# Two layers and a set of transposes put on 64-column tiles of TensorE, the shape that the projections beside them have

## The chip, the cores and the metric

The kernel runs on one core of a Trainium2 chip. The metric is device microseconds (us) of one execution. The span that a profile counts is about 2 us shorter than the timed execution. A time is called fast state where repeated executions agree within 1.5% and the granted clock is full; a single run of a one-core program has no state that could be told, and I use single runs below only for what their traces show or for differences far larger than the scatter.

## The reference

Attention with projected keys and values (Linformer), then a two-layer network on its output. There are 8 batches with 8 heads, 1024 positions and 64 values per head.

```python
k_proj = einsum('ks,bhsd->bhkd', E, k)            # 1024 positions -> 64
v_proj = einsum('ks,bhsd->bhkd', F, v)
attn   = softmax(q @ k_proj^T / 8) @ v_proj
x = attn.transpose(0, 2, 1, 3).reshape(8192, 512)
h = x @ w_in                                       # 512 -> 2048
g = h * clip(h + 3, 0, 6) / 6
out = g @ w_out                                    # 2048 -> 512, float32
```

## The kernel before

Inputs are cast to bf16 on their way in; sums are kept in f32 in PSUM. Each batch is two blocks of 512 tokens. The order of instructions on every engine is fixed by hand: the second layer of one block alternates with the first layer of the next, and the attention of the next batch is put between them in small pieces. TensorE's work has three main shapes: the layers use the full array (128 rows x 128 columns), the projections use two tiles of 128 x 64, and scores, values and most sums of attention use tiles of 64 x 64 (some sums use 128 x 32, and the first transposes of the keys 64 x 128). These are the parts that the change touches:

```python
def project(self, alloc):                 # 128x64, two column tiles in turn
    ps = self.ps = alloc()
    for so in range(SO):                  # SO = 8
        for e in range(2):                # 0: keys by E, 1: values by F
            nc.tensor.matmul(ps[e * KP:(e + 1) * KP], ef_t[e][:, so, :],
                             kqv[self.b]["kv"[e]][:, :, so, :],
                             start=(so == 0), stop=(so == SO - 1))
...
def queries(self, t, js):                 # first batch only
    ...
    nc.tensor.transpose(ps[:, o:o + P], q0[...], ident)
...
def h_part(h_ps, xT, t, fo, kos):         # first layer, 128x128
    for ko in kos:
        nc.tensor.matmul(h_ps, w_in_sb[:, ko, fo * P:(fo + 1) * P], xT[:, ko, t, :],
                         start=(ko == 0), stop=(ko == KO - 1))
...
def second_group(b, t, g, c, copy=None):  # second layer, 128x128
    ...
    for fo in range(FO):                  # FO = 16
        nc.tensor.matmul(o_ps, g[:, fo, c * P:(c + 1) * P], w_out_sb[:, fo, :],
                         start=(fo == 0), stop=(fo == FO - 1))
        if fo % SB == SB - 1:
            yield                         # attention may be put in here
```

Three more places matter for the experiments: the warm-up of TensorE at the start, the transfers that bring keys and queries into the layout for the scores, and where the next batch's work is put into the schedule of the first batch:

```python
busy(12)                                  # 12 matmuls of 512 columns on ones, before any data
...
def turn(self):                           # a transfer that transposes
    nc.sync.dma_start_transpose(self.kT, self.kp.rearrange("p h a d -> p (h a d)"))
    ...
    qT_dma[self.b] = q_transposed(self.b)
    ...
    nc.gpsimd.tensor_copy(mark, last)     # waits for qT; then the next batch is loaded
    load_kqv(self.b + 1, ...)
...
for fo in range(2, FO):
    first_group(xT, 1, g[1], fo)
    pop()
    if fo == 7:
        second.projected()                # projections of batch 1, and turn() afterwards
    ...
...
for c in range(SB):
    for i, _ in enumerate(second_group(0, 1, g[1], c, nc.vector.tensor_copy)):
        pop()
        if i == 0:
            rest.append(second.visit(c, None))   # visit(0): scores of batch 1
        ...
```

The softmax here doesn't subtract the row's maximum and nothing guards it: scores larger than these inputs give would overflow.

## Time and profile before

The first three runs gave a median of 507.31 us (507.19 to 507.36).

| | before |
|---|---|
| span in the profile | 505.3 us, granted clock 1.0 |
| TensorE busy | 495.5 us, 98% |
| ScalarE / VectorE busy | 256.2 us (51%) / 245.3 us (49%) |
| data moved | 66 MB, 131 GB/s on average |

In the lines of the profile PE is TensorE's matmuls, PEld its weight loads, DVE VectorE, ACT ScalarE, POOL GpSimd and SP SyncE; L532 is a line of the kernel, `a<-b` a tile and what it is made from, 128\*64 the rows and columns of the array that are used. The prediction below shows the lines for TensorE. Two more lines of the page of before also belong here. The first is the mean busy share of the 16 DMA engines in 40 slices of the span (in tenths, one slice is 12.6 us); the second is the queue on which TensorE's instructions come in: packets, MB, share of 16 engines.

```profile
DMA  9999989699199998699217990248110361101112
...
q8 instruction: 21, 0.34, 0.3%
```

In the first 80 us nearly every slice is at 9: the DMA engines have hardly a pause, so I take it that the transfers of that time land as late as the bandwidth makes them. The second line looks like nothing, and I read it so.

The view of the waits of TensorE in before (who waited for whom: us in total, times, longest) has six entries, of which these are the last three:

```profile
PE at L414 <- ACT vp L385: 0.5, 1, 0.5
PE mm L407 <- DVE kT L377: 0.3, 1, 0.3
PE mm L532 <- DVE g L503: 0.2, 1, 0.2
```

None of the six is a wait for a transfer. What the list doesn't say is by how little a transfer was in time.

### The profile page before, as it was taken

The numbers are of one execution on the slowest core, as the hardware profiler recorded it, in microseconds if no ns is written. First come the engines' busy times: TensorE is split into PE (matmuls) and PEld (weight loads), VectorE is DVE, ScalarE is ACT, GpSimd is POOL, SyncE is SP. The second block draws the span as 40 slices with busy tenths as digits, with TensorE's granted clock in tenths as the row PEclk, the third lists the DMA queues.
The fourth block names the chain that finished last, engine by engine and source line by source line (L and its number), as shares of the span: only waits on it lengthen the run. The fifth ranks groups of instructions, "written<-read, shape, count | busy, mean of one in ns | idle before, by whom it ended". The sixth has DMA issues, their size and how long they took to land.

```text
span 505.3 us, 7033 instructions
## 1 busy us (share of the span) xinstructions
PE 495.5 (98%) x2728; PEld 224.9 (45%) x2778; DVE 245.3 (49%) x384; ACT 256.2 (51%) x438; POOL 38.7 (8%) x58
## 2 busy tenths in 40 slices
PE   8899999999999999999999999999999999999997
PEld 4444444444444444444444444444444444444444
DVE  3572736855733573526635455533752446334420
ACT  3757476567574444654555544654455544434431
POOL 8620020010020020010002000000000000000000
PEclk9999999999999999999999999999999999999999
DMA  9999989699199998699217990248110361101112
GB/s 168 198 205 208 195 154 231 123 162 204 61 159 198 260 153 161 137 169 257 98 43 134 215 263 28 62 97 209 42 43 30 82 162 43 40 24 42 43 42 83
DMA packets 78057, 66.02 MB, mean 131 GB/s; under 512 B 36216, under 2 KB 67192, under 8 KB 78024
## 3 DMA queue, kind: packets, MB, share of 16 engines
q0 software_dynamic: 32480, 29.36, 37.1%
q1 hardware_dynamic: 45320, 35.89, 27.1%
q8 instruction: 21, 0.34, 0.3%
q10 hardware_dynamic: 224, 0.33, 0.3%
q14 instruction: 12, 0.10, 0.1%
HBM read 69.73 MB, written 16.94 MB: 172 GB/s over the span
## 4 chain that ended last, share of the span: by engine, by line
PE 97%; ACT 1%; issue 1%; DVE 0%; ACTq 0%
PE mm L532 43%; PE mm L497 43%; PE at L195 2%; PE mm L93 1%; PE at L244 1%; PE at L226 1%; PE mm L244 1%; PE mm L524 1%; PE mm L264 1%; PE at L414 1%; ACT aT L235 0%; PE mm L226 0%; PE at L382 0%; PE at L394 0%; PE mm L195 0%
## 5 line engine op out<-in xcount | busy, mean ns | idle before, releaser
L503 DVE SCALAR_TENSOR_TENSOR g<-r,mm 128x512 bf16<-128x512 f32 x256 | 173.6, 687 | 178.9 <-ACT r L502 178.1
L497 PE MATMUL mm<-xT,w_in_sb 128*128 128x512 bf16 x997 | 229.0, 379 | 1.5
L532 PE MATMUL mm<-w_out_sb,g 128*128 128x512 bf16 x985 | 227.8, 379 | 1.9 <-issue 1.0
L502 ACT ACTIVATE r<-mm 128x512 f32<-128x512 f32 x256 | 152.3, 599 | 74.5 <-PE mm L497 73.2
L497 PEld LDWEIGHTS <-w_in_sb 128*128 128x128 bf16 x1024 | 99.5, 98 | 122.2 <-issue 3.3
L532 PEld LDWEIGHTS <-g 128*128 128x128 bf16 x1008 | 96.7, 98 | 120.6 <-issue 7.4
L537 ACT COPY o_sb<-mm 128x512 f32<-128x512 f32 x55 | 32.3, 587 | 126.6 <-PE mm L532 123.7
L257 DVE TENSOR_TENSOR xT<-at,rec 128x512 bf16<-128x512 f32 x42 | 26.5, 682 | 6.4 <-ACT rec L176 6.4
L235 ACT ACTIVATE aT<-at 128x512 bf16<-128x512 f32 x38 | 20.2, 615 | 9.1 <-PE at L226 9.1
L201 DVE CAST kp<-at 64x512 bf16<-64x512 f32 x12 | 7.7, 677 | 15.5 <-PE at L195 15.5
L216 POOL COPY mark<-qT 1x1 bf16<-1x1 bf16 x4 | 0.7, 176 | 161.9 <-DMA qT<-q 161.9
L235 ACT ACTIVATE aT<-mm 128x512 bf16<-128x512 f32 x18 | 10.3, 613 | 3.6 <-PE mm L226 3.6
L537 DVE COPY o_sb<-mm 128x512 f32<-128x512 f32 x8 | 5.5, 688 | 13.4 <-PE mm L532 13.4
L195 PE MATMUL at<-k,e_t 128*64 128x512 bf16 x48 | 11.5, 382 | 0.0
L195 PE MATMUL at<-v,f_t 128*64 128x512 bf16 x48 | 11.5, 381 | 0.0
L257 DVE TENSOR_TENSOR xT<-mm,rec 128x512 bf16<-128x512 f32 x14 | 9.0, 686 | 4.3 <-PE mm L244 4.3
L176 ACT ACTIVATE rec<-rec 128x1024 f32<-128x1024 f32 x10 | 10.6, 1060 | 0.3
L170 ACT ACTIVATE rec<-mm 128x512 f32<-128x512 f32 x10 | 5.5, 595 | 7.9 <-PE mm L244 5.4
L170 ACT ACTIVATE few<-mm 128x512 f32<-128x512 f32 x10 | 5.4, 595 | 7.4 <-PE mm L264 7.4
L93 PE MATMUL mm<-ones 128*128 128x512 bf16 x18 | 7.4, 549 | 1.5 <-DVE halves L84 1.5
L204 DVE CAST vp<-at 64x512 bf16<-64x512 f32 x12 | 8.3, 694 | 0.4
L195 PEld LDWEIGHTS <-e_t 128*64 128x64 bf16 x56 | 5.6, 109 | 6.2 <-issue 1.9
(75 smaller groups left out, 161.0 us busy)
## 6 DMA issues: line engine op xcount, KB each, us to landing
out_dram<-o_sb SPq DMA_DIRECT2D x63, 256.0 KB, 2.5
rec<-rows SPq DMA_DIRECT2D x40, 256.0 KB, 6.2
k<-in_k_dram POOLq DMA_DIRECT2D x7, 1024.0 KB, 14.1
v<-in_v_dram POOLq DMA_DIRECT2D x7, 1024.0 KB, 20.9
q<-in_q_dram POOLq DMA_DIRECT2D x7, 1024.0 KB, 10.7
w_out_sb<-in_moe_w_out_dram POOLq DMA_DIRECT2D x4, 512.0 KB, 16.3
w_in_sb<-in_moe_w_in_dram POOLq DMA_DIRECT2D x5, 256.0 KB, 9.8
k<-in_k_dram POOLq DMA_DIRECT2D x4, 256.0 KB, 5.6
```

The costliest lines, as they stand in the source:

```text
L93: nc.tensor.matmul(ps, ones[:, :P], ones, start=True, stop=True)
L170: nc.scalar.activation(rec[:, i], den, AF.Ln)
L176: nc.scalar.activation(flat, flat, AF.Exp, scale=-1.0)
L195: nc.tensor.matmul(ps[e * KP:(e + 1) * KP], ef_t[e][:, so, :], kqv[self.b]["kv"[e]][:, :, so, :], start=(so == 0), stop=(so == SO - 1))
L235: nc.scalar.activation(self.aT[j][:, r].rearrange("p a n -> p (a n)"), tiles[r], AF.Exp, scale=scale)
L244: nc.tensor.matmul(tiles[t][c:c + D].rearrange("p (r n) -> p r n", r=2), stationary(r, 2 * j + a), self.aT[j][r:r + KP, :, a, :], start=Tr ...
L257: nc.vector.tensor_mul(self.xT[:, j, t, :], av[t], rec[:, t])
L497: nc.tensor.matmul(h_ps, w_in_sb[:, ko, fo * P:(fo + 1) * P], xT[:, ko, t, :], start=(ko == 0), stop=(ko == KO - 1))
L502: nc.scalar.activation(r, h_ps, AF.Relu, bias=0.5, scale=1.0 / 6.0)
L503: nc.vector.scalar_tensor_tensor(g[:, fo, :], r, 1.0, h_ps, op0=ALU.min, op1=ALU.mult)
L532: nc.tensor.matmul(o_ps, g[:, fo, c * P:(c + 1) * P], w_out_sb[:, fo, :], start=(fo == 0), stop=(fo == FO - 1))
L537: (copy or nc.scalar.copy)(o_sb, o_ps)
```

## The change

The intent is to save the cost of switching TensorE between shapes. Layers and second-block transposes take the shape that the projections have: every full-width product is split into two of 64 columns, written to the two halves of the same PSUM tile. The work of the array stays the same; the number of TensorE instructions goes up by three quarters.

```diff
+    width = [P // 2]
+
+    def in_columns(ps, stationary, moving, **flags):
+        for lo in range(0, stationary.shape[-1], width[0]):
+            nc.tensor.matmul(ps[lo:lo + width[0]], stationary[:, lo:lo + width[0]], moving, **flags)
...
# project
-                    nc.tensor.matmul(ps[e * KP:(e + 1) * KP], ef_t[e][:, so, :], ...
+                    in_columns(ps[e * KP:(e + 1) * KP], ef_t[e][:, so, :], ...
...
# queries
-                        nc.tensor.transpose(ps[:, o:o + P], q0[...], ident)
+                        n = width[0] if t else P
+                        for lo in range(0, P, n):
+                            nc.tensor.transpose(ps[lo:lo + n, o:o + P], q0[...][:, lo:lo + n], ident)
...
# h_part
-            nc.tensor.matmul(h_ps, w_in_sb[:, ko, fo * P:(fo + 1) * P], xT[:, ko, t, :],
+            in_columns(h_ps, w_in_sb[:, ko, fo * P:(fo + 1) * P], xT[:, ko, t, :],
...
# second_group, in both of its loops
-            nc.tensor.matmul(o_ps, g[:, fo, c * P:(c + 1) * P], w_out_sb[:, fo, :],
+            in_columns(o_ps, g[:, fo, c * P:(c + 1) * P], w_out_sb[:, fo, :],
```

## The prediction

> **What bounds the kernel now.** I read the page first: which engine is full, and what the chain that ended last consists of.
>
> ```profile
> PE 495.5 (98%) x2728; PEld 224.9 (45%) x2778; DVE 245.3 (49%) x384; ACT 256.2 (51%) x438; POOL 38.7 (8%) x58
> ...
> PE 97%; ACT 1%; issue 1%; DVE 0%; ACTq 0%
> ...
> L497 PE MATMUL mm<-xT,w_in_sb 128*128 128x512 bf16 x997 | 229.0, 379 | 1.5
> L532 PE MATMUL mm<-w_out_sb,g 128*128 128x512 bf16 x985 | 227.8, 379 | 1.9 <-issue 1.0
> ...
> L497 PEld LDWEIGHTS <-w_in_sb 128*128 128x128 bf16 x1024 | 99.5, 98 | 122.2 <-issue 3.3
> ```
>
> TensorE is the bound: 98% busy, 97% of the chain, and its two layer groups wait 1.5 and 1.9 us in all. Other engines have about half their time free. So only what changes the rhythm of TensorE's own stream counts. The 379 ns is the modelled duration of one overlapping matmul; the rhythm is the distance of starts. Between layer matmuls that follow each other it is 215.8 ns (mean of 1887 distances). A weight load (98 ns) fits beneath.
>
> Next I looked for a place where the old kernel already runs what the new one will run everywhere. The projections of keys and values are that: two matmuls of 128 rows and 64 columns, one writing partitions 0 to 63 of the PSUM tile and one 64 to 127. This is TensorE's timeline around one of them: start, length, instruction, count.
>
> ```profile
> 129.68 1.03 PE L532 MATMUL mm<-w_out_sb,g 128*128 128x512 bf16 x4
> 130.64 0.40 PE L244 MATMUL mm<-aT,ones 64*64 64x512 bf16 x2
> ...
> 131.09 0.39 PE L244 MATMUL at<-aT,vp 64*64 64x512 bf16 x4
> 131.41 0.40 PE L195 MATMUL at<-k,e_t 128*64 128x512 bf16 x1
> 131.41 0.40 PE L195 MATMUL at<-v,f_t 128*64 128x512 bf16 x1
> 131.65 0.38 PE L195 MATMUL at<-k,e_t 128*64 128x512 bf16 x1
> 131.65 0.38 PE L195 MATMUL at<-v,f_t 128*64 128x512 bf16 x1
> ...
> 132.94 0.38 PE L195 MATMUL at<-k,e_t 128*64 128x512 bf16 x1
> 132.95 0.38 PE L195 MATMUL at<-v,f_t 128*64 128x512 bf16 x1
> 133.26 1.25 PE L497 MATMUL mm<-xT,w_in_sb 128*128 128x512 bf16 x4
> ```
>
> Two things are to be seen. The halves of a pair start within 4 ns of each other and pairs follow at 216 ns (131.65 to 132.94 is six steps): a pair costs what one full matmul costs. And at each change of shape a step is longer: 131.09 to 131.41 (64*64 to 128*64) and 132.94 to 133.26 (128*64 to 128*128) are 0.31 to 0.32 us in place of 0.216. Over all clean changes of shape in the trace, the first load of the new shape starts 88 to 92 ns later than the rhythm would have it (112 in some early ones), whatever the two shapes. I take 91 ns per change.
>
> The loads of the same stretch:
>
> ```profile
> 131.65 0.11 PEld L195 LDWEIGHTS <-e_t 128*64 128x64 bf16 x1
> 131.66 0.11 PEld L195 LDWEIGHTS <-f_t 128*64 128x64 bf16 x1
> 131.87 0.11 PEld L195 LDWEIGHTS <-e_t 128*64 128x64 bf16 x1
> 131.87 0.11 PEld L195 LDWEIGHTS <-f_t 128*64 128x64 bf16 x1
> ```
>
> Both loads of the next pair run side by side, 110 ns, under the running pair.
>
> **What the Trainium skill says.** "TensorEngine Tiling (Array Packing)", Key Properties: changing the tiling mode drains the array, and tiles work independently, loads too. The trace agrees: 91 ns per change, pairs in step. The same page, Restrictions, says that column tiling disables Fast Weight Load. The trace fits: a 64-column load takes 110 ns, a full one of twice the columns 98. "TensorE: Matmul & The Clock Gate", "Wait — 56ns, not 53.3ns?", gives some 62 ns of sequencer time per MATMUL if decoding in hardware is off; that is the danger here, see the rivals. "Runtime: NRT & Kernel Launch", Instruction fetch mechanics: instructions come in 16 KiB blocks of 256; the trace shows 21 such packets on the instruction queue, about 1 us each.
>
> **The change, part by part.** From the order of instructions: TensorE goes from 2778 to 4858 matmuls, each with a load; 2064 layer matmuls and 16 transposes are halved. Other engines keep their instructions and order. The projections stay as they are, since they were already 64 wide.
>
> 1. Layer slots. 1024 of the first layer and 1008 of the second, each 512 wide, go from one matmul at 215.8 ns to a pair. The projections' pairs step at 215 to 216 ns: change 0, at most 0.2 ns x 2032 = 0.4 us.
>
> 2. Changes of shape. I counted them in program order: 100 before, 91 after. Three projections stand between layers and lose two changes each; four stand between 64*64 work and layers and lose one each; one is added where the first block's values (still 128*128) meet the first layer matmul. Net 9, by 91 ns: -0.8 us, all on TensorE's path. The transposes of the second block stand among layer matmuls; halving them costs nothing by itself and saves the four changes that they would otherwise have brought.
>
> 3. Entry into a shape. After a change, the first step of a 64-wide pair is 240 ns (131.41 to 131.65), 24 over the rhythm; that of a full shape is 226, 10 over. Entries into 128*64 grow from 11 to 33, into 128*128 fall from 42 to 11: 22 x 24 - 31 x 10 = +0.2 us.
>
> 4. Short slots. The last output tile has 16 matmuls 384 wide and 16 only 128 wide; these with the 16 transposes, also 128 wide, have some 56 ns per slot. Two loads of 64 columns go under that only if they truly run at once; if one follows the other at, say, the 55.7 ns step which the first block's 64-column loads keep, each of 32 slots doubles: +1.8 us at worst, I put in +0.2.
>
> 5. Loads, queues, semaphores. DVE and ACT are released by the second half of the last pair, 2 to 4 ns later. No new wait of TensorE is on something recent: the few waits on its own semaphore reach 62 or more instructions back. Instruction blocks double in number, to roughly 38 in all, one per 14 us instead of 28, at 1 us each and fetched ahead.
>
> Sum: -0.8 + 0.2 + 0.2 = -0.4 us on 507.31: 506.9 us.
>
> **The rivals.** *Issue becomes the bound.* Four instructions must now be handed over per 216 ns, 54 ns each, for 440 us on end; a projection needs only 32, and the queue can have gathered those. If each took 62 ns, a slot would be 248 ns: 2032 x 32 = +65 us, 572 us. Against it: at 67.24 us a semaphore instruction of the sequencer, in front of the scores, finished its wait (51 ns long), and the 24 loads behind it had begun by 68.56 with 23 matmuls between them: 47 instructions in 1.27 us, 27 ns each, twice the needed speed. This supposes that the sequencer hands over nothing past that wait; it is also a burst, not a stream. This is my main doubt.
>
> *Loads no longer fit.* If the two loads of a pair ran one after the other, 220 ns would exceed 216: +4 ns x 2032 = +8 us, 515 us. Against it: they start 2 to 4 ns apart and the pairs hold 216.
>
> *Halves do not overlap, or collide in PSUM.* That would nearly double the time; the projections write the two halves of one bank in the same way and show nothing of it.
>
> *The drain gets cheaper.* If leaving 64 columns for 64*64 and back cost less than leaving the full array, the 50-odd changes left in the body would shrink too: up to 5 us, 502 us. Against it: 64*64 to 128*64 shows 88 to 89 ns, 128*64 to 64*64 91 to 92, as the others.
>
> *Another engine takes over.* ACT and DVE are half idle and get no work: no.
>
> **Range and chances.** What is certain is small, under 1 us each way. Short slots can add 1.6, and chips differ by some tenths: 505.7 to 508.8 us. Issue or loads failing in the long stream is outside it; I give that 7%. Faster by 2% needs 10 us, more than all the changes of shape cost together (100 x 91 ns = 9.1 us): 1%.
>
> **What would show it.** Right: layer pairs starting 215 to 216 ns apart throughout; 91 changes of shape at some 91 ns; loads of 110 ns, TensorE's load row up in busy time though hidden; DVE and ACT unchanged. Wrong: steps of 220 ns or more inside long layer stretches (issue or loads), idle TensorE ended by "issue" that grows with the length of the stretch, stops at every 256th instruction (fetching), or a last output tile longer than its 3.5 us.

## The result and the profile after

| | before | after |
|---|---|---|
| median, with lowest and highest of 6 runs each | 507.32 us (507.19 to 507.92) | 507.30 us (506.89 to 507.38) |
| ratio of fast runs | | 0.9996, 95% interval 0.9983 to 1.0009 |
| span in the profile | 505.3 us | 505.5 us |

A ratio is the mean time of one kernel's fast runs over the mean time of the other's fast runs of the same rounds, so it is not quite the ratio of the two medians. The change did nothing that can be measured in the time. The prediction of 506.9 us, with a range of 505.7 to 508.8, holds. What is left is to see whether it holds for its reasons: it had asked for -0.4 us, and the traces differ by +0.2.

The page of after, with the lines that answer to those of the prediction. One helper now issues projections and layers, so that both are line 172 (the transposes have a line of their own, 403).

```profile
PE 498.9 (99%) x4858; PEld 259.5 (51%) x4858; DVE 245.1 (48%) x384; ACT 256.1 (51%) x438; POOL 38.7 (8%) x58
...
q8 instruction: 38, 0.62, 0.5%
...
PE 85%; DMA 12%; POOL 2%; ACT 1%; issue 0%; DVE 0%; ACTq 0%; POOLq 0%
...
L172 PE MATMUL mm<-w_out_sb,g 128*64 128x512 bf16 (+2 forms) x2080 | 235.0, 376 | 0.2 <-DVE g L512 0.2
L172 PE MATMUL mm<-xT,w_in_sb 128*64 128x512 bf16 x2048 | 231.5, 379 | 0.3
...
L172 PEld LDWEIGHTS <-w_in_sb 128*64 128x64 bf16 x2048 | 117.2, 110 | 104.0 <-issue 0.8
```

TensorE is as full as it was, DVE and ACT are the same, the layer groups wait even less than before (0.2 and 0.3 us in place of 1.9 and 1.5), and the loads of 110 ns were hidden. One line is new in kind: 12% of the chain that ended last is now DMA, where before it was none. A chain follows one releaser at each step, so a short wait for a transfer brings the whole history of that transfer into it; the 12% are not 60 us of waiting, but they say that somewhere TensorE did wait for a transfer.

The main stretch, in TensorE's timeline of after (start, length, instruction, count): the end of a projection, and the layers behind it.

```profile
203.81 0.38 PE L172 MATMUL at<-k,e_t 128*64 128x512 bf16 x1
203.81 0.38 PE L172 MATMUL at<-v,f_t 128*64 128x512 bf16 x1
204.03 3.62 PE L172 MATMUL mm<-xT,w_in_sb 128*64 128x512 bf16 x32
207.48 3.62 PE L172 MATMUL mm<-w_out_sb,g 128*64 128x512 bf16 x32
210.93 1.89 PE L172 MATMUL mm<-xT,w_in_sb 128*64 128x512 bf16 x16
```

Sixteen pairs take 207.48 - 204.03 = 3.45 us, 216 ns each, and 16 more the same. The step from the projection to the layer is 0.22 us, where the prediction's lines of before had 0.32 at such a place: the change of shape is gone, as it was meant to be. The short slots of the very last output tile are the last thing in the timelines of both kernels, before:

```profile
498.60 3.66 PE L524 MATMUL mm<-w_out_sb,g 128*128 128x384 bf16 x32
```

and after:

```profile
498.82 3.66 PE L172 MATMUL mm<-w_out_sb,g 128*64 128x384 bf16 x64
```

Both take 3.66 us, so 64 loads with some 56 ns per pair in half of them cost nothing. But the tile begins 0.22 us later. Since shapes became cheaper, something else must have become dearer. The view of TensorE's waits in after has two entries that before did not have:

```profile
PE at L172 <- DMA v<-in_v_dram: 0.3, 1, 0.3
...
PE mm L233 <- DMA qT<-q: 0.3, 1, 0.3
```

Both belong to batch 1, and both can be followed. First its projections, in TensorE's timeline of before:

```profile
54.80 0.40 PE L195 MATMUL at<-k,e_t 128*64 128x512 bf16 x1
54.88 0.38 PE L195 MATMUL at<-v,f_t 128*64 128x512 bf16 x1
...
56.70 0.82 PE L497 MATMUL mm<-xT,w_in_sb 128*128 128x512 bf16 x2
```

and of after:

```profile
54.70 0.38 PE L172 MATMUL at<-k,e_t 128*64 128x512 bf16 x1
55.42 0.38 PE L172 MATMUL at<-v,f_t 128*64 128x512 bf16 x1 [0.34 <-DMA v<-in_v_dram]
...
56.95 0.38 PE L172 MATMUL mm<-xT,w_in_sb 128*64 128x512 bf16 x1
```

After begins the projection 0.10 us earlier, since it has no change of shape to make. Then the first product with v starts 0.72 us behind the first with k, where it was 0.08 before; and the layer that follows starts 0.25 us later than before, although its own change of shape is saved too.

The scores of batch 1 are next. In the full timeline of before (PEld is a weight load; the copy on POOL is a marker that waits for the same transposed q as the scores do):

```profile
66.86 0.74 PEld L532 LDWEIGHTS <-g 128*128 128x128 bf16 x4
...
67.27 0.18 POOL L216 COPY mark<-qT 1x1 bf16<-1x1 bf16 x1 [36.40 <-DMA qT<-q]
...
68.03 0.64 PEld L226 LDWEIGHTS <-kT 64*64 64x64 bf16 x24 [0.42 <-issue]
```

and of after:

```profile
67.10 0.94 PEld L172 LDWEIGHTS <-g 128*64 128x64 bf16 x8
...
68.72 0.18 POOL L223 COPY mark<-qT 1x1 bf16<-1x1 bf16 x1 [38.01 <-DMA qT<-q]
68.77 0.50 PEld L233 LDWEIGHTS <-kT 64*64 64x64 bf16 x20 [0.73 <-issue]
```

The four slots of the second layer and the change of shape took 68.03 - 66.86 = 1.17 us before, and 68.77 - 67.10 = 1.67 us after. In before q had landed 0.8 us ahead of its use. In after it landed 1.45 us later, and the scores start as soon as it is there.

I then aligned the starts of all weight loads of the two traces, slot by slot (a slot is one full-width matmul, or the pair of halves that stands in its place), and looked where their distance grows. This is my own calculation from the records:

| | us |
|---|---|
| first block | -0.03 |
| changes of shape saved (three projections between layers 0.228 each, four with 64x64 work on one side 0.106 each) | -1.11 |
| longer first step of layers behind 64x64 work (24 times 13 to 14 ns) | +0.32 |
| wait for v at the projections of batch 1 | +0.47 |
| wait for transposed q at the scores of batch 1 | +0.46 |
| a step inside the scores of batch 2, at 139 us | +0.10 |
| sum | +0.21 |

The last output ends 0.23 us later; the rhythm of the layer slots is 215.8 ns before and after. So the change gained 0.8 us and lost 1.0. The step at 139 us stands where a PSUM buffer is reused; that this buffer is the cause is argued and not tested.

Why is q late? In the records of single DMA packets a packet of 16 KiB on the instruction queue takes some 1 us, in the middle of the transfers that transpose q. In after this packet runs from 65.2 to 66.2 us; 120 of the last 128 packets of the transposes have ended by 65.67, and the other eight follow only between 66.2 and 67.17. The records name no engine; eight packets of 128 are the share of one of 16, so I take it that this one engine was held by the fetch. In before all packets are done at 65.95, and no fetch lies there: in the first 140 us the fetches of before lie 18 to 22 us apart, those of after 10 to 17. (The times of this paragraph, those in the expectations, and those of fetches, landings and markers from here on count from the first weight load, which is 1.45 us after the start of the page's clock; the lines of the profile keep the page's clock. Packets and instructions are recorded apart: without a fetch the marker's start stands up to 0.2 us ahead of the last packet's end.)

That gives the theory for the experiments: *the doubled instructions are free on TensorE, but their fetches and TensorE's own earliness meet transfers that were just in time, and these give the gain back.* Its rivals: (J) the two waits are jitter of the transfers, and another run of the same kernel shows others; (I) instruction handling does have a price which the saved changes hide; (D) a part of the gain was never there.

### The profile page after: what moved, and what is told of

Its sections match the earlier page's. It is cut to its first block, busy times and chain, and to the rows that moved or that the text cites. A ratio compares the mean times of both kernels' runs of the same rounds, so it can differ in the third digit from the quotient of the medians.

```text
span 505.5 us, 11242 instructions
## 1 busy us (share of the span) xinstructions
PE 498.9 (99%) x4858; PEld 259.5 (51%) x4858; DVE 245.1 (48%) x384; ACT 256.1 (51%) x438; POOL 38.7 (8%) x58
## 4 chain that ended last, share of the span: by engine, by line
PE 85%; DMA 12%; POOL 2%; ACT 1%; issue 0%; DVE 0%; ACTq 0%; POOLq 0%
PE mm L172 79%; DMA q<-in_q_dram 6%; DMA w_in_sb<-in_moe_w_in_dram 2%; PE at L172 2%; DMA v<-in_v_dram 2%; DMA qT<-q 2%; PE at L251 1%; PE at L233 1%; PE mm L251 1%; POOL q L106 1%; PE mm L271 1%; POOL k L110 1%; ACT aT L242 0%; PE mm L233 0%; POOL v L110 0%
## 5 line engine op out<-in xcount | busy, mean ns | idle before, releaser
L172 PE MATMUL mm<-w_out_sb,g 128*64 128x512 bf16 (+2 forms) x2080 | 235.0, 376 | 0.2 <-DVE g L512 0.2
L172 PE MATMUL mm<-xT,w_in_sb 128*64 128x512 bf16 x2048 | 231.5, 379 | 0.3
L172 PEld LDWEIGHTS <-w_in_sb 128*64 128x64 bf16 x2048 | 117.2, 110 | 104.0 <-issue 0.8
L172 PEld LDWEIGHTS <-g 128*64 128x64 bf16 x2080 | 116.2, 110 | 105.5 <-issue 7.0
```

The costliest lines, as they stand in the source:

```text
L172: nc.tensor.matmul(ps[lo:lo + width[0]], stationary[:, lo:lo + width[0]], moving, **flags)
```

## The experiments

Each call ran its kernels on one chip together with runs of the kernel before; the ratios are to those.

### Both kernels once more: e1 and e2

No edit but a blank line.

> The kernel before, unchanged, for a second trace. Theory F (instruction fetching): each 16 KiB block of TensorE's instructions occupies one DMA engine for about 1 us and delays what shares that engine; the place of the blocks is fixed by the program. Then this trace repeats the first: block fetches at 34.6 and 57.0 us after the first weight load, the projection of batch 1 waiting under 0.1 us for v, the scores of batch 1 waiting 0 for the transposed q. Rival J (jitter of DMA from run to run): the waits differ from the first trace by several tenths of a us.

The kernel before: 507.9 us in one run. Its scores had no wait for q (marker at 65.90 us, 65.82 in the first trace), but its projections of batch 1 waited 0.41 us for their inputs, without any fetch near.

> The changed kernel, unchanged, for a second trace. Theory F: block fetches again at 53.1 and 65.2 us after the first load, and again some 0.45 us of wait for v at the projection of batch 1 and some 0.45 us for the transposed q in front of its scores, within 0.15 us. Rival J: one or both waits gone or twice as long.

The kernel after: 507.3 us in one run, and both waits came again, in the same places: 0.3 us for v, 0.2 us for q, with the fetch at 65.2 and the marker at 67.30.

What follows: the wait for q belongs to the change, since two traces of each kernel agree. The wait for v is partly rival J: v lands within 53.4 to 54.0 us in these four traces, TensorE comes for it between 53.0 and 53.5, and the old kernel can meet it as well.

### The fetches moved: e3 and e4

A fetch comes about every 256 instructions (the kernel after has 38 fetches for 9716 loads and matmuls). More and smaller warm-up matmuls at the start shift all later fetches and take the same time.

```diff
 # e3, on the kernel after
-    busy(12)
+    ps0 = pmm()
+    for _ in range(96):
+        nc.tensor.matmul(ps0[:, :64], ones[:, :P], ones[:, :64], start=True, stop=True)
```

> The changed kernel with the 12 warm-up matmuls of 512 columns written as 96 of 64 columns: the same columns, 168 more instructions ahead of everything, so that the block fetches come some 9 us earlier in the stream, at about 44, 56 and 69 us, clear of the landing of v (53.4) and of the end of the transposes of q (59 to 66). Theory F: both waits fall to under 0.15 us together and the kernel ends 0.6 to 0.9 us sooner than the changed one, about 506.5 us. Rival J, or a delay that comes from the volume of fetching and not from its place: the waits stay, 507.3 us.

Measured: 506.73 us (506.68 to 507.15), ratio 0.9983 (0.9968 to 0.9998). The fetches lie at 57.1 and 70.4 us, none in the transposes of q; those are done by 66.08, the marker is back at 65.89, and both waits of batch 1 are gone from the list. For q that is so. For v it is not quite: v landed at 54.10, with no fetch near, and its first product still started 0.40 us behind the first with k, in overlap with a running matmul, so that the list, which counts idle time over 0.15 us, does not show it. By the aligned traces some 0.2 us of that wait are left. In their place stands this entry, the second of TensorE's waits:

```profile
PE at L375 <- DMA k<-in_k_dram: 1.3, 2, 1.1
```

A fetch at 7.7 us now meets the first keys. The aligned traces put the net loss of it at some 0.4 us, since part of this wait would have been spent anyway. So the wait for q follows the fetch, and moving fetches takes from one transfer what it gives to another. The other traces agree: in the six of the kernel after and its variants that have a fetch between 64.8 and 65.7 us (after, e2, e6, e7, e10, e12) the last eight packets of q end 1.3 to 1.6 us behind the others, in the seven traces with none there (before, e1, e3, e4, e5, e8, e9) 0.1 us. (e11, which runs at another pace, is left out.)

```diff
 # e4, on the kernel before
-    busy(12)
+    ps0 = pmm()
+    for _ in range(30):
+        nc.tensor.matmul(ps0[:, :205], ones[:, :P], ones[:, :205], start=True, stop=True)
```

> The kernel before with the warm-up as 30 matmuls of 205 columns in place of 12 of 512: 36 more instructions, which moves its fetch at 57.0 us to about 53.2 us, onto the landing of v, and the next from 75 to about 71. Theory F: the projection of batch 1 now waits 0.3 to 0.6 us for v, as in the changed kernel, though all layers are full width; the scores still wait for nothing; the time 0 to 0.5 us above before. Rival J: no wait for v, 507.3 us.

Measured: 509.01 us (508.57 to 509.67), ratio 1.0023 (1.0007 to 1.0040). The shot missed its target: a fetch fell at 54.1, and no wait for v came of it. But another one, at 137.8 us, fell onto the end of the transposes of the keys of batch 2, and TensorE's longest wait is now there:

```profile
PE mm L228 <- DMA kT<-kp: 1.6, 1, 1.6
```

The data were done at 137.5 us, but the last two packets, of 4 bytes each, went only at 138.65, as the fetch ended. Of the 16 semaphore signals that tell of this transfer's end, fifteen came between 137.88 and 138.01 and the last at 139.84; the scores started at 139.88. In the first trace of the kernel before the fetch comes at 137.9, when the packets of kT are done since 136.5. This is the clearest case: the kernel *before*, with 36 more instructions ahead of all its work, is 0.2% slower, and of the 2.6 us by which the span of its profiled run is longer, 1.6 stand at one fetch. Another 1.1 us or so come from waits in the first block and for w_out, and I have not followed those one by one; for v, a fetch at that place made no wait.

### Only the first layer in columns: e5

```diff
 # second_group, main loop
-            in_columns(o_ps, g[:, fo, c * P:(c + 1) * P], w_out_sb[:, fo, :],
-                       start=(fo == 0), stop=(fo == FO - 1))
+            nc.tensor.matmul(o_ps, g[:, fo, c * P:(c + 1) * P], w_out_sb[:, fo, :],
+                             start=(fo == 0), stop=(fo == FO - 1))
```

> The changed kernel with the second layer back on the full array and the first layer still on 64-column tiles, so that the array changes shape at each alternation of the layers: 198 changes of shape in place of 91. Theory S (a change costs 91 ns wherever it stands, plus 24 ns on the first step of a 64-column run and 10 on that of a full run): 107 x 91 ns = 9.7 us, entries 28 x 24 + 78 x 10 = 1.5 us, together 11.2 us: 518.5 us, range 517 to 519.5. Rival: between 128 rows by 64 columns and the full array the drain is hidden in a dense stream, or weights can be loaded across the change: under 512 us.

Measured: 518.2 us (517.81 to 518.4), ratio 1.0214 (1.0200 to 1.0228), where I had expected 518.5. TensorE's timeline:

```profile
206.70 3.62 PE L172 MATMUL mm<-xT,w_in_sb 128*64 128x512 bf16 x32
210.25 3.63 PE L541 MATMUL mm<-w_out_sb,g 128*128 128x512 bf16 x15
213.81 1.49 PE L172 MATMUL mm<-xT,w_in_sb 128*64 128x512 bf16 x12
```

Sixteen slots of either kind now take 3.55 and 3.56 us in place of 3.45: one change each. The kernel has 198 changes, 107 more than after, and (516.4 - 505.5) / 107 = 102 ns for each, the longer first step included. This trace has neither of the two waits of batch 1 (its fetches lie elsewhere), so the changes cost up to 0.9 us more than the two spans differ by: 102 to 111 ns each, where I had reckoned 105. So the price of a change is about what I took it for, and the 0.8 us that the change of this study saved are real (rival D falls for this term). It also shows that all of it must move together: half of this change costs 2%.

### 32-column tiles: e6

```diff
-    width = [P // 2]
+    width = [P // 4]
```

> The changed kernel on 32-column tiles: four matmuls and four loads in each 216 ns, 27 ns per instruction, 86 changes of shape. Theory: tiles run side by side, loads too, and issue is fast enough: 507 us, 505.5 to 509, with the same 216 ns rhythm. Rival issue: a sequencer that needs more than 27 ns per instruction sets the rhythm; at 35 ns a slot would be 280 ns and the time about 637 us. It finds the margin that the 64-column kernel has: if this one holds 216 ns, the margin is at least twofold. The blocks of instructions double again, so the waits behind fetches may add some tenths.

Measured: 507.63 us (507.49 to 511.06, four runs), ratio 1.0023 (0.9997 to 1.0049); three of the four lie at 507.5 to 507.7. The page's first line:

```profile
PE 498.4 (99%) x9130; PEld 246.5 (49%) x9130; DVE 245.2 (48%) x384; ACT 256.2 (51%) x438; POOL 38.7 (8%) x58
```

The rhythm is 215.8 ns per slot with eight instructions in each, four loads and four matmuls: 27 ns each, for 440 us. Rival I falls: four per slot, as in the kernel after, are half of what TensorE takes without a trace of it. The fetches are now 71, and the two waits stand there as after (0.9 and 0.4 us at the longest).

### Slack in place of moved fetches: e7, e8 and, for a check, e12

If the gain is given back because the projections and the scores of batch 1 come as early as their inputs, then they should come a little later, with layer work put in front of them: the projections one group of the first layer later, the first scores four slots later.

```diff
-        if fo == 7:
+        if fo == 8:
             second.projected()
...
-            if i == 0:
+            if i == (1 if c == 0 else 0):
                 rest.append(second.visit(c, None))
```

> The changed kernel with the projection of batch 1 one layer group later and the scores of batch 1 four slots later, 0.86 us each, so that v and the transposed q have landed. Theory G (the gain of the change, about 0.8 us, was given back at two transfers that land just in time): the waits for v and q vanish, and the time falls by 0.6 to 0.9 us, to 506.4 to 506.7 us. Rival: the waits come back elsewhere, for example at the first sums of batch 1, whose exponentials then have less time: 507.3 us.

The kernel after with slack: 506.65 us (506.27 to 506.88), ratio 0.9988 (0.9975 to 1.0000). Neither wait is in the list of TensorE's waits:

```profile
PE mm L93 <- DVE halves L84: 1.5, 1, 1.5
PE mm L416 <- DVE kT L384: 0.3, 1, 0.3
PE at L373 <- DMA k<-in_k_dram: 0.3, 1, 0.3
PE mm L423 <- ACT aT L443: 0.3, 1, 0.3
PE mm L172 <- DVE g L512: 0.2, 1, 0.2
```

In the trace the first products with k and v start together again. The fetch is still in the transposes (at 65.7 us, marker 67.77), and the scores start 0.06 us after the marker, without having waited: the slack was just enough. By the aligned traces the two places give back 1.04 us. This one profiled run lost some 0.7 us in its first block at half clock (mean clock 0.997), so its span of 505.1 shows less.

> The same two moves in the kernel before, as the control. In its first trace it waited under 0.1 us for v and not for q, in the second 0.4 us for v: 0 to 0.4 us faster than before. Theory G wants the changed kernel with slack to be 0.4 to 0.8 us under this one. Rival: no difference between the two, because the full-array kernel gains as much from the slack.

The same edits on the kernel before: 507.02 us (506.94 to 507.88), ratio 0.9995 (0.9982 to 1.0009); its trace moves by -0.03 us. Slack alone does nothing, since there was no wait to take away. Between these two, on the same chip and in the same rounds, lies what the shapes are worth when nothing gives it back: 0.9988 / 0.9995, or -0.4 us, with intervals of 0.6 us and more on either side. The sign is as expected; with such intervals neither it nor the size is settled by this pair. The aligned traces are the better evidence.

> The changed kernel with the two transfers given 0.86 us of slack, once more, to firm up a difference near the noise: 506.2 to 506.9 us, 0.05 to 0.25 % under before, no wait of TensorE for v or the transposed q of batch 1. Its first trace had some 2.5 us at half the clock in the first block; without that the span should be about 504.5 us.

The kernel of e7 once more, on another chip: 506.43 us (506.05 to 506.69), ratio 0.9982 (0.9968 to 0.9996), span 504.3, full clock, again without the two waits. That is 1.2 us of span under after; by its own aligned trace 0.94 us come from the two places and 0.28 from the first block. This is the best version that I have; against before it is 0.1 to 0.2%.

### A fetch put into the transposes of the kernel before: e9

```diff
 # on the kernel before
-    busy(12)
+    ps0 = pmm()
+    for _ in range(115):
+        nc.tensor.matmul(ps0[:, :53], ones[:, :P], ones[:, :53], start=True, stop=True)
```

> The kernel before with 206 more instructions in the warm-up (115 matmuls of 53 columns for 12 of 512), which should put the block fetch of 75.3 us at about 61 us, inside the transposes of q for batch 1 (59 to 66). Theory F (a fetch holds one DMA engine for about 1 us and the transfer is done when its last engine is): the transposed q lands about 0.9 us later, at 66.7 to 67.2 us after the first load in place of 65.8, and the scores of the full-array kernel wait 0.2 to 0.6 us for it; time 507.3 to 508.2 us. Rival: only a fetch at the very end of a transfer delays it, one in its middle is caught up: landing at 65.8 to 66.1 us, no wait. The first block may wait for k as in the other shifted kernels.

Measured: 507.59 us (507.33 to 507.76), ratio 1.0006 (0.9991 to 1.0022). The fetches fell at 57.4 and 80.0 us and none near 65; the marker stayed at 65.86, and there was no wait. I had reckoned the place of the fetch from the number of instructions, and this did not give it. The run tells nothing of what a fetch in the transposes of q does to the kernel before; that it would have the same effect as in e4 for kT is left as argued.

### How the halves find each other: e10 and e11

Where does the pairing come from? In the kernel after, the two halves stand next to each other in the program. The first test hands the first layer over in groups of four, aaaa bbbb; the second hands the second layer over as 16 a, then 16 b.

```diff
 # e10, h_part
-        for ko in kos:
-            in_columns(h_ps, w_in_sb[:, ko, fo * P:(fo + 1) * P], xT[:, ko, t, :],
-                       start=(ko == 0), stop=(ko == KO - 1))
+        for lo in range(0, P, P // 2):
+            for ko in kos:
+                nc.tensor.matmul(h_ps[lo:lo + P // 2], w_in_sb[:, ko, fo * P + lo:fo * P + lo + P // 2],
+                                 xT[:, ko, t, :], start=(ko == 0), stop=(ko == KO - 1))
```

> The changed kernel with the halves of the first layer handed over apart: the four matmuls of columns 0 to 63, then the four of columns 64 to 127, the second layer still in pairs. Theory: matmuls start in order and two on the same columns cannot overlap, so a group of four slots takes six (only the neighbours at the two borders overlap): 1024 x 0.5 x 0.2158 = +110 us, 617 us. Rival: the queue finds the other half by itself and overlaps them: 507 us. Rival: nothing overlaps at all: +221 us, 728 us.

507.4 us in one run, two starts per 216 ns as before. My theory, that matmuls start in the order of the program and that halves four apart would therefore not overlap, fell here; its rival was right.

```diff
 # e11, second_group
-        for fo in range(FO):
-            in_columns(o_ps, g[:, fo, c * P:(c + 1) * P], w_out_sb[:, fo, :],
-                       start=(fo == 0), stop=(fo == FO - 1))
+        for n in range(2 * FO):
+            fo, lo = n % FO, n // FO * (P // 2)
+            nc.tensor.matmul(o_ps[lo:lo + P // 2], g[:, fo, c * P + lo:c * P + lo + P // 2], w_out_sb[:, fo, :],
+                             start=(fo == 0), stop=(fo == FO - 1))
-            if fo % SB == SB - 1:
+            if n % (2 * SB) == 2 * SB - 1:
                 yield
```

> The changed kernel with the halves of the second layer handed over far apart: sixteen matmuls (and loads) of columns 0 to 63, then sixteen of columns 64 to 127; the first layer in pairs. The last run showed that TensorE overlaps halves that stand four matmuls apart. Theory: it looks ahead only as far as some queue[...], so this too stays at 507 to 512 us (some loss where scores stand between the halves). Rival: it looks ahead about 16 instructions or fewer; then half or more of each run of sixteen goes alone, 1008 x 0.25 to 0.75 x 0.2158 = 54 to 163 us more, 560 to 670 us.

643.33 us in one run: (641.5 - 505.5) / 63 output tiles = 2.16 us for each, ten slots. Sixteen slots a tile would be lost if nothing overlapped. TensorE's timeline where a first-layer group (line 172) is followed in the program by a second-layer one (line 542):

```profile
440.38 0.38 PE L172 MATMUL mm<-xT,w_in_sb 128*64 128x512 bf16 x1
440.41 0.38 PE L542 MATMUL mm<-w_out_sb,g 128*64 128x512 bf16 x1
440.60 0.38 PE L172 MATMUL mm<-xT,w_in_sb 128*64 128x512 bf16 x1
440.63 0.38 PE L542 MATMUL mm<-w_out_sb,g 128*64 128x512 bf16 x1
```

Matmuls of line 542 start ahead of matmuls of line 172 that stand in front of them in the program, each set on its own half of the columns. At 94 of the 96 borders between the two layers in this trace four starts overlap so, at the other two fewer. TensorE looks ahead for the other column tile, but not far. The kernel after never needs more than a distance of one.

## Why the prediction was right or wrong

The time was right: 507.30 us for 506.9, well inside the range, and "within 2%" had the 92% that its 7% and 1% left over. By its own steps:

1. **Layer slots: right.** Change 0 as taken, 215.8 ns in both. The upper bound of 0.4 us was not needed.
2. **Changes of shape: right in kind, mis-sized by a little.** The 91 changes of the new kernel take 88 to 92 ns, early ones 112. The saving was put at 9 net changes by 91 ns, -0.8 us; the aligned traces show -1.11 us at the seven projections. Where two changes vanish, 228 ns vanish and not 182; 34 of the other 46 ns are the longer first steps of the two shapes, which I had put into the next term. The one change that is added lies in the first block, whose -0.03 us contains it.
3. **Entry into a shape: right.** 24 entries of 13 to 14 ns give +0.32 us for the layers. The prediction's +0.2 is net of the first steps that vanish. The two terms together were -0.6 and measured -0.79.
4. **Short slots: mis-sized.** I had put in +0.2 us, for fear that loads might go one after the other. They truly run side by side: 3.66 us before and after for the last tile, 0.
5. **Loads, queues, semaphores: this step failed.** It said: "No new wait of TensorE is on something recent", and of the instruction blocks "at 1 us each and fetched ahead". The first is true of waits on TensorE's own semaphore, and was read as if it covered waits on transfers. The second is true of TensorE, whose list of waits in after has none on issue; the spacing was misread (21 blocks in 505 us are one per 24 us, not 28). But a fetch is a transfer like others: its packet took 0.9 to 1.3 us in the kernel after, and the transfer that shared its engine was done only when the last share was (e4: fifteen semaphore signals by 138.01 us, the sixteenth at 139.84). In place of 0 the runs show +0.47 us at v and +0.46 us at q. For q the fetch is shown as the cause (six traces with it, seven without, e3 by moving it; e4 shows the like for kT). For v it is not: after and e2 had a fetch near it (53.1 and 53.3 us) and v landed at 53.9 and 54.0, but e10 and e12 had one just as near (53.2 and 52.9) and v landed at 53.3 and 53.0, e4 had one at 54.1 and no wait, and e1 and e3 had a wait and no fetch near, with v landing at 54.0 and 54.1; in e3 the wait for k had also made TensorE later. What is shown for v is that a later arrival ends the wait (e7, e12), against a transfer that is itself uncertain by 0.7 us; whether the fetch has a part in it stays open.

So the right total hides one error of more than twice the effect that was predicted: predicted -0.4 us, measured about +0.2 between the traces and -0.02 between the medians. Shapes gave 0.2 us more than reckoned, short slots cost 0.2 us less, and the three waits cost 1.0 us that were not in the sum. The range held because its allowance for "chips differ by some tenths" covered what I had not thought of; so far the total was right by luck.

Of the rivals, issue as the bound fell for good with e6 (27 ns per instruction, kept up for 440 us). Loads that no longer fit fell with the 110 ns beneath 216, and even with pairs in 56 ns slots. Halves that do not overlap fell at once, and e10 and e11 show why they overlap so readily. The cheaper drain fell with the 88 to 92 ns of all changes. The other engines did not change. What the list of signs lacked was a wait for a transfer; it would have shown step 5 wrong at first sight.

## What to carry to other kernels

Splitting matmuls into column tiles of one shape cost nothing in TensorE's rhythm here and saves about 0.1 us for each change of shape that vanishes, so count the changes before writing it: nine fewer are not worth it, while 107 more cost 2%. A gain on the busiest engine is kept only where its next inputs are already there; look in the old trace for transfers that land within a microsecond of their use, and move work in front of them together with the change. More instructions also mean more instruction fetches on the same DMA engines as the data, which matters only for transfers that are just in time.

## What the Trainium skill lacked or had wrong

- "Runtime: NRT & Kernel Launch", Instruction fetch mechanics, calls crossing a block boundary "mostly hidden". It lacks that the block's packet can hold up data on the DMA engines: each 16 KiB packet took about 1 us (0.9 to 1.3 in the kernel after), put off transposed q by 1.4 us in the kernel after, and made a wait of 1.6 us for kT in e4.
- "TensorE: Matmul & The Clock Gate", The mechanism, says that matmuls start in strict program order and, in its list of what overlaps, that loads overlap running matmuls only where the row group differs (the text above the list also allows a background weight buffer). Here matmuls of the other column tile started up to four ahead and out of program order (e10: 507.4 us with halves four apart; e11's lines 542 and 172), and loads on the same rows ran under matmuls throughout (110 ns beneath 216).
- The same page, Back-to-back issue gap, gives about 131 ns per matmul of 512 columns as the sustained rate of a stream with loads. The layers ran at 215.8 ns before and after; the page's formula for the isolated gap fits. Its note of 62 ns per MATMUL without decoding in hardware did not apply: e6 kept up 54 ns per load and matmul.
- "TensorEngine Tiling (Array Packing)", Key Properties, says that a change of tiling mode drains TensorE, but gives no cost: 88 to 92 ns here for every pair of shapes, 102 to 111 ns with the longer first step (e5).
